# Softcap attention and MLP: q and k loaded in 128-byte runs and turned in 32x32 blocks on VectorE, scores as single float32 products, tokens in natural order

## The chip, the cores and the metric

The kernel runs on one NeuronCore of one Trainium2 chip. The metric is the time of one execution on the device, in microseconds. The kernel before has a median of 661.09 us over three runs (660.58 to 662.39).

## What is computed

Four batches of twelve heads, 448 tokens, 64 numbers per head. Attention with a soft cap on the scores, then an MLP with a squared ReLU over the 1792 tokens (768 wide, 2048 hidden). Cut to what matters:

```
scores = (1 / sqrt(64)) * q @ k.T              # q, k, v: (4, 12, 448, 64) float32
scores = cap * tanh(scores / cap)              # cap = 30
attn = exp(scores - max)                       # softmax over the keys
attn = attn / (sum(attn) + 1e-9)
x = (attn @ v), heads side by side             # (1792, 768)
h = maximum(x @ w_in, 0)                       # w_in (768, 2048), w_out (2048, 768): 8-byte floats
out = (h * h) @ w_out                          # (1792, 768) float32
```

## The kernel before, in words

Work is done by pairs of heads: 24 pairs (`NP`), six for each batch. The two heads of a pair lie in the upper and the lower 64 partitions of the array, so that one instruction of ScalarE or VectorE serves both, and a product for the one head can run on the row tiles beside that for the other.

**Loads.** `load_q`, `load_k` and `load_v` (L334 to L347) fetch one pair with four DMAs each. A head's 448 tokens are cut as 64 groups of 7 neighbours, (p t) with t = 7; group p goes to partition p, four of its seven tokens in one half of the partitions and three in the other. On the tile's side each token is a run of 64 floats, 256 bytes. This is why tokens stand in the order `ORDER` (L202), and why `put` (L752) writes each result block as two DMAs of 64 rows seven tokens apart. q is issued from SyncE (SP), k and v from GpSimd (POOL).

**Turning.** `transpose_k` and `transpose_q` (L357, L363) turn k and q with eight TensorE transposes of 128x128 into PSUM: k into a bank of `ps_t`, q into the second half of the score tile `half`. `take` (L369) then splits each into a rounded float32r part (`kqh`) and the rest (`kql`), four VectorE operations for a pair.

**Scores.** `scores(n, u)` (L378) makes scores of pair n with the keys on the partitions and the 448 queries as columns. Units u = 1, 2, 3 hold 128 keys of each head, on two row tiles of 64; unit 0 holds the last 64 keys of both heads in one product over 128 rows, where zeros that `prepare` wrote keep the heads apart. Each unit is three float32r products (hi hi, hi lo, lo hi), which add up to a float32 one. The score tiles come from `ps_s`, which has two buffers: scores(n, 0) and the transposes of q need the buffer that the tanh of scores(n, 1) reads, scores(n, 3) that of scores(n, 2).

**The rest of a pair.** `tanh` and `exp` on ScalarE (L392, L397). Then, one pair behind: `pv_half` (L404), the products with v and with ones for unit 0, four float32 products on the four 64x64 quarters of the array; `sums` (L414), the row sums; `pv` (L421), the six products with v of units 1 to 3; `evac` (L428) on ScalarE. `take_sums`, `invert`, `spread` and `normalise` bring the reciprocal of the sums back through DRAM by DMAs of SyncE and write x as a float32r part and a rest.

**The order.** Through the whole attention stage the order on each engine and queue is written out by hand in the loop at L534. For pair n TensorE does: scores 1 and 2; the transposes of pair n + 1; scores 0; from pair 9 on one part of the first MLP product (`part`, six matmuls of L309); scores 3; pv_half, sums and pv of pair n - 1. ScalarE does: tanh 1, tanh 2, exp 1, exp 2, a step of decoding, tanh 3, tanh 0, exp 3, exp 0, a step of decoding, evac. The decoding turns 8-byte weights into float32r pairs (L30), a step at a time, and fetches the weights from the SyncE queue (L272) behind the loads of q. Loads for pair n + 2 are issued in pair n, into one of two buffers (four for v).

After the 24 pairs come the rest of the first MLP product (L309, until about 443 us), whose order a planner sets, and the second (L748) by a seven-product scheme, in an order written by hand.

Of the kernel before, what the change touches and what calls it, by code (L numbers as in the profile page):

```python
# [10 lines left out]
F32 = mybir.dt.float32  # L11
F32R = mybir.dt.float32r
# [176 lines left out]
def tile_softcap_attention_mlp(ctx, tc, q, k, v, cap, w_in, w_out, out):  # L189
    nc = tc.nc  # L190
    B, H, S, D = q.shape
    NT, DM = out.shape
    DFF = w_in.shape[1]
    P = 128
    NS = S // D
    NPAIR = H // 2
    NP = B * NPAIR
    KDM = DM // P
    NF = DFF // P
    HO = DM // 2  # L200
# [6 lines left out]
    NKQ = 2  # L207
    NKV = 4
# [12 lines left out]

    hpad = rctx.enter_context(tc.tile_pool(name="hpad", bufs=1))
    hpad.tile([P, 16], F32, name="hpad")
    qp = rctx.enter_context(tc.tile_pool(name="qp", bufs=2))
    wpool = wctx.enter_context(tc.tile_pool(name="w", bufs=NEARLY, side="right"))
    scr = wctx.enter_context(tc.tile_pool(name="scr", bufs=1, side="right"))
    ps_m = rctx.enter_context(tc.tile_pool(name="ps_m", bufs=1, space=PSUM))
# [18 lines left out]

    kn = [keep.tile([P, 4, 2, D], F32, name=f"kn{i}") for i in range(NKQ)]
    qn = [keep.tile([P, 4, 2, D], F32, name=f"qn{i}") for i in range(NKQ)]  # L250
    vn = [keep.tile([P, 2, 4, D], F32, name=f"vn{i}") for i in range(NKV)]

    ones = keep.tile([P, 2, 32], F32, name="ones")
    zero = keep.tile([P, P], F32, name="zero")

    def prepare():

        for t in kn:
            nc.vector.memset(t[D:P, 3, 0], 0.0)
            nc.vector.memset(t[0:D, 3, 1], 0.0)  # L260
        for t in qn:
            nc.vector.memset(t[D:P, 3], 0.0)
        nc.vector.memset(ones[:, 0], 1.0)
        nc.vector.memset(ones[:, 1], 0.0)

# [17 lines left out]
            yield from decode_f64(nc, pool, raw, hi[:, o:o + HO], lo[:, o:o + HO], HO, bufs)  # L283

    def hold_win(f, pool, tags):
        win[f] = tuple(pool.tile([P, 4 * P + S], F32R, tag=t, name=t)[:, :DM] if tags == LATE else
                       pool.tile([P, DM], F32R, tag=t, name=t) for t in tags)
        return win[f]

    EARLY, LATE = ("whi", "wlo"), ("kqh", "kql")  # L290

    def load_wout(f, pool, scratch):
        hi = pool.tile([P, DM], F32R, tag="ohi", name="ohi")
# [30 lines left out]

    top, bottom = slice(0, D), slice(D, P)

    def load_keys(dst, src, n, queues):
        b, j = divmod(n, NPAIR)
        for i, at in enumerate((4, 3)):
            x = src[b, 2 * j + i].rearrange("(p t) d -> p t d", t=NS)  # L330
            yield queues[i].dma_start(out=dst[top, 0:at, i], in_=x[:, 0:at])  # L331
            yield queues[i].dma_start(out=dst[bottom, 0:NS - at, i], in_=x[:, at:NS])

    def load_k(n, queues=(nc.sync, nc.sync)):  # L334
        for _ in load_keys(kn[n % NKQ], k, n, queues):
            pass

    def load_q(n, upper=(nc.sync, nc.sync), lower=None):
        b, j = divmod(n, NPAIR)
        for i in range(2):  # L340
            x = q[b, 2 * j + i].rearrange("(p t) d -> p t d", t=NS)
            upper[i].dma_start(out=qn[n % NKQ][top, 0:4, i], in_=x[:, 0:4])
            (lower or upper)[i].dma_start(out=qn[n % NKQ][bottom, 0:3, i], in_=x[:, 4:7])  # L343

    def load_v(n):
        for _ in load_keys(vn[n % NKV].rearrange("p h t d -> p t h d"), v, n, (nc.gpsimd, nc.gpsimd)):
            pass  # L347
# [6 lines left out]
    kqs, tps, probs, adds, pvs, es, rds = {}, {}, {}, {}, {}, {}, {}


    def transpose_k(n):  # L357
        tps[n, 0] = ps_t.tile([P, 512], F32, tag="t", name="tp")
        kf = kn[n % NKQ].rearrange("p t h d -> p t (h d)")
        for t in range(4):  # L360
            nc.tensor.transpose(tps[n, 0][:, t * P:(t + 1) * P], kf[:, t], ident)  # L361

    def transpose_q(n, tp):  # L363
        tps[n, 1] = tp
        qf = qn[n % NKQ].rearrange("p t h d -> p t (h d)")
        for t in range(4):
            nc.tensor.transpose(tp[:, t * P:(t + 1) * P], qf[:, t], ident)  # L367

    def take(n, i, cast=nc.vector.tensor_copy):  # L369
        cols = (slice(0, 4 * P), slice(4 * P, 4 * P + S))[i]  # L370
        if i == 0:
            kqs[n] = [qp.tile([P, 4 * P + S], F32R, tag=x, name=x) for x in LATE]
        hi, lo = kqs[n]
        tp = tps.pop((n, i))[:, :cols.stop - cols.start]
        cast(out=hi[:, cols], in_=tp)
        nc.vector.tensor_sub(out=lo[:, cols], in0=tp, in1=hi[:, cols].bitcast(F32))

    def scores(n, u, sc=None):  # L378
        hi, lo = kqs[n]
        if sc is None:  # L380
            sc = ps_s.tile([P, 2, 512], F32, tag="s", name="sc")
        rows, t = ((top, bottom), u - 1) if u else ((slice(0, P),), 3)
        for s, (kx, qx) in enumerate(((hi, hi), (hi, lo), (lo, hi))):
            for h, r in enumerate(rows):
                nc.tensor.matmul(out=sc[:, h, :S], lhsT=kx[r, t * P:(t + 1) * P], rhs=qx[r, 4 * P:],  # L385
                                 start=(s == 0), stop=(s == 2))
        probs[n, u] = sc

    def tanh(n, u):
# [14 lines left out]
    def pv_half(n):  # L404
        pvs[n, 0] = ps_v.tile([P, S], F32, tag="pa", name="pa")
        pvs[n, 1] = ps_v.tile([P, S], F32, tag="pb", name="pb")
        p = probs.pop((n, 0))[:, 0]
        for h, (r, o) in enumerate(((top, bottom), (bottom, top))):
            nc.tensor.matmul(out=pvs[n, 0][r], lhsT=vn[n % NKV][r, h, 3], rhs=p[r], start=True, stop=False)  # L409
# [11 lines left out]
    def pv(n):  # L421
        for u in range(1, NU):
            p = probs.pop((n, u))
            for h, r in enumerate((top, bottom)):
                nc.tensor.matmul(out=pvs[n, 0][r], lhsT=vn[n % NKV][:, h, u - 1], rhs=p[:, h],  # L425
                                 start=False, stop=(u == NU - 1))

    def evac(n):  # L428
# [41 lines left out]
    warm = ps_t.tile([P, 512], F32, tag="t", name="warm")  # L470
    for _ in range(NWARM):
        nc.tensor.matmul(out=warm[:, :P], lhsT=zero, rhs=zero, start=True, stop=True)
    make_identity(nc, ident)
    load_k(0, (nc.sync, nc.scalar))
    load_q(0, (nc.gpsimd, nc.scalar), (nc.gpsimd, nc.sync))
    nc.gpsimd.dma_start(out=cap_sb, in_=cap.partition_broadcast(P))
    load_k(1)
    load_q(1, (nc.gpsimd, nc.gpsimd))
    prepare()
    load_v(0)  # L480
    load_v(1)
# [52 lines left out]
    for n in range(NP + 1):  # L534
        on, prep, old = n < NP, n + 1 < NP, n > 0
        more = n + 2 < NP

        if on:
            scores(n, 1)
            scores(n, 2)  # L540
            tanh(n, 1)
            tanh(n, 2)
            exp(n, 1)
            exp(n, 2)
        if more:
# [12 lines left out]
        if on:
            scores(n, 0, half)
        if prep:  # L560
            take(n + 1, 0)
            take(n + 1, 1)
        if on and parts[0][1] in decoded and n >= NPAIR * (parts[0][0] + 1) + 3:
            part()
        if n >= 2:
            invert(n - 2)

        if on:
            scores(n, 3)
            tanh(n, 3)  # L570
            tanh(n, 0)
            exp(n, 3)
            exp(n, 0)

        if old:
            pv_half(n - 1)
            sums(n - 1)
        if on:
            add_p(n)
        if old:  # L580
            take_sums(n - 1)
            pv(n - 1)
        if n >= 3:
# [128 lines left out]
    with ExitStack() as mctx:  # L712
# [189 lines left out]
```

## Time and profile before

| | us |
|---|---|
| median of three runs | 661.09 |
| the profiled execution | 661.23 |
| its span, first to last instruction | 659.5 |
| TensorE matmuls busy | 642.3 |
| VectorE busy | 477.1 |
| ScalarE busy | 355.9 |
| GpSimd busy | 113.8 |
| mean granted TensorE clock, of full | 0.993 |

An engine's busy time counts the stretches in which one of its instructions is under way. Matmuls are pipelined and their ends are modelled, so that two that follow each other overlap, and a TensorE that is shown as busy is not one that gives out results at its peak. Of the chain of work that ended last, 94% is on TensorE; 35% of the span is the first MLP product, 30% the second, 12% scores, 2% the transposes of k and 14% the products with v and the sums.

### The profile page before, as it was taken

To read this page: it belongs to the slowest core of one execution; us is meant where nothing else is said; L and a number is where in the kernel's file an instruction comes from. 1 tells how busy PE (TensorE), PEld (TensorE's weight loads), DVE (VectorE), ACT (ScalarE), POOL (GpSimd) and SP (SyncE) were. 2 spreads that over 40 slices of the span, in tenths; PEclk is the share of its full clock that TensorE was granted. 3 is DMA by queue.
4 is the path that set the end of the run, shared out by engine and by line. 5 is a ranking of instruction groups with operands and counts; after the bars stand their busy time and mean duration, and the time that the engine had idled before them with its cause. 6 is when DMAs were issued, how large, how long until landed. Compare 5 with 4: busy or idle time off the path is not lost.

```text
span 659.5 us, 10469 instructions
## 1 busy us (share of the span) xinstructions
PE 642.3 (97%) x3714; PEld 522.6 (79%) x3714; DVE 477.1 (72%) x860; ACT 355.9 (54%) x498; POOL 113.8 (17%) x201
## 2 busy tenths in 40 slices
PE   6999999999999999999999999998999999999995
PEld 5444455545554599999999999998999999999995
DVE  4678878967887456279889998913989987666651
ACT  5998988978788431355557555533444442222220
POOL 8655555534540010000000000000000000000000
PEclk9999999999999999999999999998999999999999
DMA  7346454546532251366576878729979905666611
GB/s 180 93 114 139 114 131 116 145 94 152 136 100 54 58 185 62 111 206 205 178 218 191 255 238 260 227 89 340 240 191 280 291 25 163 164 165 163 164 38 40
DMA packets 134300, 104.07 MB, mean 158 GB/s; under 512 B 40064, under 2 KB 126592, under 8 KB 134240
## 3 DMA queue, kind: packets, MB, share of 16 engines
q1 hardware_dynamic: 127376, 92.23, 49.5%
q0 software_dynamic: 6112, 10.91, 6.4%
q8 instruction: 31, 0.51, 0.3%
q10 hardware_dynamic: 752, 0.18, 0.1%
q14 instruction: 29, 0.24, 0.1%
HBM read 79.69 MB, written 23.42 MB: 156 GB/s over the span
## 4 chain that ended last, share of the span: by engine, by line
PE 94%; DMA 2%; SPq 1%; ACT 1%; DVE 1%; issue 0%; DVEq 0%
PE hps L309 35%; PE po L748 30%; PE sc L385 10%; PE pa L425 8%; PE pb L417 3%; PE pa L409 3%; PE tp L361 2%; PE sc L367 2%; DMA a<-g_dram 1%; DMA wraw<-in_moe_w_in_dram 1%; DMA qn<-in_q_dram 1%; ACT p L392 0%; SPq L318 0%; SPq L343 0%; DVE gl L738 0%
## 5 line engine op out<-in xcount | busy, mean ns | idle before, releaser
L309 PE MATMUL hps<-xs,kqh 128*128 128x448 f32 x576 | 163.5, 364 | 0.0
L748 PE MATMUL po<-th,gh 128*128 128x384 f32 x392 | 132.4, 338 | 1.6 <-ACT gh L737 1.6
L748 PE MATMUL po<-th,gl 128*128 128x384 f32 x392 | 132.6, 338 | 0.6 <-DVE gl L738 0.6
L748 PE MATMUL po<-tl,gh 128*128 128x384 f32 x392 | 132.2, 337 | 0.0
L737 ACT CAST gh<-a 128x1024 fp32r<-128x1024 f32 x49 | 51.5, 1052 | 121.3 <-PE po L748 95.7
L309 PEld LDWEIGHTS hps<-xs,kqh 128*128 128x128 f32 x576 | 108.1, 188 | 7.5
L309 PE MATMUL hps<-xs,kql 128*128 128x448 f32 x288 | 104.5, 363 | 0.0
L392 ACT ACTIVATE p<-sc,qks 128x896 f32<-128x896 f32 x96 | 82.5, 911 | 12.7 <-PE sc L385 12.6
L397 ACT ACTIVATE p<-p,cap_sb 128x896 f32<-128x896 f32 x96 | 85.7, 948 | 0.0
L738 DVE TENSOR_TENSOR gl<-a,gh 128x1024 fp32r<-128x1024 f32 x49 | 59.9, 1223 | 35.5 <-DMA a<-g_dram 22.7
L313 ACT ACTIVATE r<-hps 128x448 f32<-128x448 f32 x64 | 34.7, 542 | 76.4 <-PE hps L309 74.3
L748 PEld LDWEIGHTS po<-th,gh 128*128 128x128 f32 x392 | 74.2, 189 | 1.9 <-ACT gh L737 1.9
L748 PEld LDWEIGHTS po<-th,gl 128*128 128x128 f32 x392 | 74.0, 189 | 1.0 <-DVE gl L738 1.0
L748 PEld LDWEIGHTS po<-tl,gh 128*128 128x128 f32 x392 | 74.2, 189 | 0.0
L425 PE MATMUL pa<-p,vn 128*64 128x448 f32 x288 | 59.4, 548 | 0.0
L309 PEld LDWEIGHTS hps<-xs,kql 128*128 128x128 f32 x288 | 53.9, 187 | 5.2
L309 PE MATMUL hps<-xs,whi 128*128 128x448 f32 x192 | 54.3, 363 | 0.0
L401 DVE TENSOR_TENSOR add<-p 128x896 f32<-128x896 f32 x24 | 26.2, 1092 | 34.1 <-PE pb L417 34.1
L425 PEld LDWEIGHTS pa<-p,vn 128*64 128x64 f32 x288 | 18.5, 136 | 39.8 <-issue 39.8
L385 PE MATMUL sc<-kqh 64*128 64x448 f32 (+1 forms) x168 | 42.5, 439 | 4.6 <-ACT p L392 4.0
L385 PEld LDWEIGHTS sc<-kqh 64*128 64x128 f32 (+1 forms) x168 | 18.1, 186 | 28.7 <-ACT p L392 7.7
L331 POOL DMA_DIRECT2D vn<-in_v_dram x48 | 26.0, 541 | 82.3 <-PE pa L425 82.3
(99 smaller groups left out, 1006.4 us busy)
## 6 DMA issues: line engine op xcount, KB each, us to landing
a<-g_dram SPq DMA_DIRECT2D x56, 512.0 KB
g_dram<-r SPq DMA_DIRECT2D x64, 224.0 KB
wraw<-in_moe_w_in_dram SPq DMA_DIRECT2D x32, 384.0 KB
wraw<-in_moe_w_out_dram SPq DMA_DIRECT2D x32, 384.0 KB
rb<-rd SPq DMA_DIRECT2D x48, 112.0 KB
out_dram<-osb SPq DMA_DIRECT2D x56, 96.0 KB
vn<-in_v_dram POOLq DMA_DIRECT2D x48, 64.0 KB, 2.6
w_dram<-part SPq DMA_DIRECT2D x16, 192.0 KB
```

The source lines that it names most:

```text
L309: nc.tensor.matmul(out=ps, lhsT=w[:, c * P:(c + 1) * P], rhs=x[b, c], start=(n == 0), stop=(n == 3 * KDM - 1))
L313: nc.scalar.activation(out=r, in_=ps, func=ACTF.Relu)
L331: yield queues[i].dma_start(out=dst[top, 0:at, i], in_=x[:, 0:at])
L385: nc.tensor.matmul(out=sc[:, h, :S], lhsT=kx[r, t * P:(t + 1) * P], rhs=qx[r, 4 * P:], start=(s == 0), stop=(s == 2))
L392: nc.scalar.activation(out=p, in_=probs[n, u][:, :c, :S], func=ACTF.Tanh, scale=qks)
L397: nc.scalar.activation(out=p, in_=p, func=ACTF.Exp, scale=cap_sb)
L401: nc.vector.tensor_add(out=adds[n], in0=probs[n, 1], in1=probs[n, 2])
L409: nc.tensor.matmul(out=pvs[n, 0][r], lhsT=vn[n % NKV][r, h, 3], rhs=p[r], start=True, stop=False)
L425: nc.tensor.matmul(out=pvs[n, 0][r], lhsT=vn[n % NKV][:, h, u - 1], rhs=p[:, h], start=False, stop=(u == NU - 1))
L737: nc.scalar.copy(out=hi, in_=x)
L738: nc.vector.tensor_sub(out=lo, in0=x, in1=f32(hi))
L748: nc.tensor.matmul(out=po, lhsT=w[:, c], rhs=m[:, cols], start=(c == 0 and i == 0), stop=(c == HF - 1 and i == 2))
```

## The change

It changes how q and k are loaded, turned and multiplied, and with that the order of the tokens.

- q and k of a pair lie in one tile `kqn` of 128 partitions. `load_kq` fetches k or q with four DMAs of 32 partitions: each takes half of a head's 64 numbers (32 floats, 128 bytes), token 32 t + r to partition r. q stays on SyncE and k on GpSimd in the loop.
- `turn_kq` turns all 32x32 blocks of k and q at once, with one VectorE transpose of 128x896, into `kq`; the eight TensorE transposes and the four operations of `take` are gone.
- `scores` makes each unit as one float32 product per head. Units 1 to 3 take every third key, `kt[r, u - 1:3 * P:3]`, as the stationary operand; unit 0 is two products of 64x64, each on the rows and the columns of its own half.
- v is loaded with three DMAs: three neighbouring tokens (768 bytes) to a partition, and the last 64 tokens of each head.
- `put` writes a result block as one DMA of 128 rows.
- At the start the first loads are issued before the identity is made, and v of pair 0 comes before k and q of pair 1. The pool `qp` has four buffers of one tag where it had two of two tags.

The core of the diff:

```diff
-    def load_keys(dst, src, n, queues):
+    def load_kq(n, i, *queues):
         b, j = divmod(n, NPAIR)
-        for i, at in enumerate((4, 3)):
-            x = src[b, 2 * j + i].rearrange("(p t) d -> p t d", t=NS)
-            yield queues[i].dma_start(out=dst[top, 0:at, i], in_=x[:, 0:at])
-            yield queues[i].dma_start(out=dst[bottom, 0:NS - at, i], in_=x[:, at:NS])
+        for a in range(4):
+            h, w = divmod(a, 2)
+            x = (k, q)[i][b, 2 * j + h, :, 32 * w:32 * w + 32].rearrange("(t r) e -> r t e", r=32)
+            queues[a % len(queues)].dma_start(out=kqn[n % NKQ][32 * a:32 * a + 32, i], in_=x)
...
+        x, dst = v[b, 2 * j:2 * j + 2], vn[n % NKV]
+        nc.gpsimd.dma_start(out=dst[:, 0:6].rearrange("p (h u) d -> p h u d", h=2),
+                            in_=x[:, 0:3 * P].rearrange("h (p u) d -> p h u d", u=3))
+        for h, r in enumerate((top, bottom)):
+            nc.gpsimd.dma_start(out=dst[r, 6], in_=x[h, 3 * P:])
...
-    def scores(n, u, sc=None):
-        hi, lo = kqs[n]
-        if sc is None:
-            sc = ps_s.tile([P, 2, 512], F32, tag="s", name="sc")
-        rows, t = ((top, bottom), u - 1) if u else ((slice(0, P),), 3)
-        for s, (kx, qx) in enumerate(((hi, hi), (hi, lo), (lo, hi))):
-            for h, r in enumerate(rows):
-                nc.tensor.matmul(out=sc[:, h, :S], lhsT=kx[r, t * P:(t + 1) * P], rhs=qx[r, 4 * P:],
-                                 start=(s == 0), stop=(s == 2))
+    def turn_kq(n):
+        kqs[n] = qp.tile([P, 2 * S], F32, tag="kq", name="kq")
+        nc.vector.transpose(out=kqs[n], in_=kqn[n % NKQ].rearrange("p i t e -> p (i t e)"))
+
+    def scores(n, u):
+        sc = ps_s.tile([P, 2, 512], F32, tag="s", name="sc")
+        kt, qt = kqs[n][:, :S], kqs[n][:, S:]
+        for h, r in enumerate((top, bottom)):
+            if u:
+                w = kt[r, u - 1:3 * P:3]
+                nc.tensor.matmul(out=sc[:, h, :S], lhsT=w, rhs=qt[r], start=True, stop=True)
+            else:
+                nc.tensor.matmul(out=sc[r, 0, :S], lhsT=kt[r, 3 * P:], rhs=qt[r], start=True, stop=True)
...
-    make_identity(nc, ident)
-    load_k(0, (nc.sync, nc.scalar))
-    load_q(0, (nc.gpsimd, nc.scalar), (nc.gpsimd, nc.sync))
-    nc.gpsimd.dma_start(out=cap_sb, in_=cap.partition_broadcast(P))
-    load_k(1)
-    load_q(1, (nc.gpsimd, nc.gpsimd))
+    load_kq(0, 0, nc.sync, nc.scalar)
+    load_kq(0, 1, nc.sync, nc.scalar, nc.gpsimd, nc.gpsimd)
+    nc.gpsimd.dma_start(out=cap_sb, in_=cap.partition_broadcast(P))
+    load_v(0)
+    load_kq(1, 0, nc.gpsimd)
+    load_kq(1, 1, nc.sync)
+    load_v(1)
+    make_identity(nc, ident)
     prepare()
-    load_v(0)
-    load_v(1)
-    transpose_k(0)
-    take(0, 0, nc.scalar.copy)
-    transpose_q(0, ps_m.tile([P, 512], F32, tag="m", name="tp"))
-    take(0, 1, nc.scalar.copy)
+    turn_kq(0)
...
         if on:
-            half = ps_s.tile([P, 2, 512], F32, tag="s", name="sc")
+            scores(n, 0)
         if prep:
-            transpose_k(n + 1)
-            transpose_q(n + 1, half[:, 1])
-        if on:
-            scores(n, 0, half)
-        if prep:
-            take(n + 1, 0)
-            take(n + 1, 1)
+            turn_kq(n + 1)
...
-            for a in range(2):
-                b, blk = divmod(2 * tt + a, NS)
-                dst = out[b * S:(b + 1) * S, o * HO:(o + 1) * HO].rearrange("(p t) e -> t p e", t=NS)[ORDER[blk]]
-                nc.sync.dma_start(out=dst, in_=osb[a * D:(a + 1) * D])
+            nc.sync.dma_start(out=out[tt * P:(tt + 1) * P, o * HO:(o + 1) * HO], in_=osb)
```

## Rows read from the trace of the kernel before

**Rows 1.** Stretches; columns: length, busy by engine (instructions), clock, DMA share, GB/s.
```profile
65.89:74.07 8.18, 8.18 (x60) 3.97 (x59) 6.33 (x13) 7.62 (x10) 4.58 (x8) 1.00 0.44 116
193.87:203.25 9.38, 9.38 (x65) 5.09 (x63) 7.15 (x15) 7.72 (x10) 2.09 (x4) 1.00 0.47 118
```
**Rows 2.** Order of time, TensorE, one pair without a part: start, length, instruction.
```profile
65.89 0.47 PE L385 MATMUL sc<-kqh 64*128 64x448 f32 x2
...
67.86 0.66 PE L367 MATMUL sc<-ident,qn 128*128 128x128 f32 x4
68.27 0.45 PE L385 MATMUL sc<-kqh 128*128 128x448 f32 x1
...
69.05 0.47 PE L385 MATMUL sc<-kqh 64*128 64x448 f32 x2
...
69.86 0.59 PE L409 MATMUL pa<-p,vn 64*64 64x448 f32 x1
...
70.28 0.54 PE L409 MATMUL pa<-p,vn 64*64 64x448 f32 x1
...
70.77 0.56 PE L417 MATMUL pb<-add,ones 128*32 128x448 f32 x1
...
71.66 2.48 PE L425 MATMUL pa<-p,vn 128*64 128x448 f32 x12
74.07 0.47 PE L385 MATMUL sc<-kqh 64*128 64x448 f32 x2
```
**Rows 3.** Order of time, ScalarE, the same pair: its first two tanh.
```profile
66.80 1.91 ACT L392 ACTIVATE p<-sc,qks 128x896 f32<-128x896 f32 x2 [0.23 <-PE sc L385]
```
**Rows 4.** Order of time, TensorE, the last pair: scores(23, 0).
```profile
214.60 0.47 PE L385 MATMUL sc<-kqh 128*128 128x448 f32 x1 [0.49 <-ACT p L392]
```
**Rows 5.** Order of time, TensorE, a pair with a part: scores 0, part, scores 3.
```profile
196.25 0.45 PE L385 MATMUL sc<-kqh 128*128 128x448 f32 x1
...
196.94 0.57 PE L309 MATMUL hps<-xs,whi 128*128 128x448 f32 x2
...
198.24 0.47 PE L385 MATMUL sc<-kqh 64*128 64x448 f32 x2
```
**Rows 6.** Instructions by line and form: busy us, mean ns, idle before.
```profile
L401 DVE TENSOR_TENSOR add<-p 128x896 f32<-128x896 f32 x24 | 26.2, 1092 | 34.1 <-PE pb L417 34.1
...
L376 DVE TENSOR_TENSOR kql<-tp,kqh 128x512 fp32r<-128x512 f32 x24 | 16.6, 691 | 5.2 <-ACT kqh L375 4.4
...
L385 PEld LDWEIGHTS sc<-kqh 64*128 64x128 f32 x144 | 13.6, 185 | 27.8 <-issue 7.5 <-ACT p L392 6.9 <-ACT p L397 3.8
...
L462 DVE CAST xs<-x 128x448 fp32r<-128x448 f32 x24 | 9.5, 394 | 0.8
```
**Rows 7.** DMA issues by line: KB each, median us from issue to landing.
```profile
kn<-in_k_dram POOLq DMA_DIRECT2D x44, 64.0 KB, 3.1
```
**Rows 8.** Stretches of the start, columns as in rows 1.
```profile
4.00:6.00 2.00, 1.90 (x10) 1.40 (x9) 0.00 (x0) 0.12 (x1) 2.00 (x5) 1.00 0.79 187
...
12.00:14.00 2.00, 0.00 (x0) 0.00 (x0) 1.26 (x3) 0.73 (x3) 2.00 (x4) 1.00 1.07 353
...
16.00:18.00 2.00, 2.00 (x13) 1.33 (x10) 1.11 (x3) 2.00 (x4) 2.00 (x4) 0.50 0.78 173
```
**Rows 9.** The chain that ended last: the start, and a later pair's scores 1, 2.
```profile
2.45 3.60 DMA qn<-in_q_dram
...
6.85 0.60 SPq L342
...
9.50 4.41 DMA wraw<-in_moe_w_in_dram
...
15.43 2.50 PE sc L385 x12
...
74.14 1.41 PE sc L385 x12
```
**Rows 10.** Order of time, SyncE's queue, the last issues.
```profile
653.31 1.10 SPq L758 DMA_DIRECT2D out_dram<-osb  x2
```

More of the change, by code (lines that the diff above doesn't have):

```diff
@@ L195, in tile_softcap_attention_mlp @@
     NS = S // D
+    NT32 = S // 32
     NPAIR = H // 2
@@ L201, in tile_softcap_attention_mlp @@
     scale = 1.0 / float(D) ** 0.5
-    ORDER = (0, 4, 1, 5, 2, 6, 3)
     NEARLY = 4
@@ L223, in tile_softcap_attention_mlp @@
     hpad.tile([P, 16], F32, name="hpad")
-    qp = rctx.enter_context(tc.tile_pool(name="qp", bufs=2))
+    qp = rctx.enter_context(tc.tile_pool(name="qp", bufs=4))
     wpool = wctx.enter_context(tc.tile_pool(name="w", bufs=NEARLY, side="right"))
@@ L243, in tile_softcap_attention_mlp @@
     ps_v = actx.enter_context(tc.tile_pool(name="ps_v", bufs=1, space=PSUM))
-    kn = [keep.tile([P, 4, 2, D], F32, name=f"kn{i}") for i in range(NKQ)]
-    qn = [keep.tile([P, 4, 2, D], F32, name=f"qn{i}") for i in range(NKQ)]
-    vn = [keep.tile([P, 2, 4, D], F32, name=f"vn{i}") for i in range(NKV)]
+    kqn = [keep.tile([P, 2, NT32, 32], F32, name=f"kqn{i}") for i in range(NKQ)]
+    vn = [keep.tile([P, NS, D], F32, name=f"vn{i}") for i in range(NKV)]
     ones = keep.tile([P, 2, 32], F32, name="ones")
@@ L256, in prepare @@
     def prepare():
[L258 to L262, printed above, removed]
         nc.vector.memset(ones[:, 0], 1.0)
@@ L285, in hold_win @@
     def hold_win(f, pool, tags):
-        win[f] = tuple(pool.tile([P, 4 * P + S], F32R, tag=t, name=t)[:, :DM] if tags == LATE else
+        win[f] = tuple(pool.tile([P, 2 * S], F32R, tag=t, name="kq")[:, :DM] if tags == LATE else
                        pool.tile([P, DM], F32R, tag=t, name=t) for t in tags)
         return win[f]
-    EARLY, LATE = ("whi", "wlo"), ("kqh", "kql")
+    EARLY, LATE = ("whi", "wlo"), ("kq", "kq")
     def load_wout(f, pool, scratch):
@@ L325, in tile_softcap_attention_mlp, with load_v @@
     top, bottom = slice(0, D), slice(D, P)
-    def load_keys(dst, src, n, queues):
+    def load_kq(n, i, *queues):
         b, j = divmod(n, NPAIR)
-        for i, at in enumerate((4, 3)):
-            x = src[b, 2 * j + i].rearrange("(p t) d -> p t d", t=NS)
-            yield queues[i].dma_start(out=dst[top, 0:at, i], in_=x[:, 0:at])
-            yield queues[i].dma_start(out=dst[bottom, 0:NS - at, i], in_=x[:, at:NS])
[L334 to L338, printed above, removed]
-        b, j = divmod(n, NPAIR)
[L340 to L347, printed above, removed]
+        for a in range(4):
+            h, w = divmod(a, 2)
+            x = (k, q)[i][b, 2 * j + h, :, 32 * w:32 * w + 32].rearrange("(t r) e -> r t e", r=32)
+            queues[a % len(queues)].dma_start(out=kqn[n % NKQ][32 * a:32 * a + 32, i], in_=x)
+    def load_v(n):
+        b, j = divmod(n, NPAIR)
+        x, dst = v[b, 2 * j:2 * j + 2], vn[n % NKV]
[3 more added lines that the diff above has]
+            nc.gpsimd.dma_start(out=dst[r, 6], in_=x[h, 3 * P:])
     NU = 4
@@ L353, in tile_softcap_attention_mlp @@
     NSCR = 2
[L354 to L372, printed above, removed]
-        hi, lo = kqs[n]
-        tp = tps.pop((n, i))[:, :cols.stop - cols.start]
-        cast(out=hi[:, cols], in_=tp)
-        nc.vector.tensor_sub(out=lo[:, cols], in0=tp, in1=hi[:, cols].bitcast(F32))
-    def scores(n, u, sc=None):
-        hi, lo = kqs[n]
-        if sc is None:
-            sc = ps_s.tile([P, 2, 512], F32, tag="s", name="sc")
-        rows, t = ((top, bottom), u - 1) if u else ((slice(0, P),), 3)
-        for s, (kx, qx) in enumerate(((hi, hi), (hi, lo), (lo, hi))):
-            for h, r in enumerate(rows):
-                nc.tensor.matmul(out=sc[:, h, :S], lhsT=kx[r, t * P:(t + 1) * P], rhs=qx[r, 4 * P:],
-                                 start=(s == 0), stop=(s == 2))
+    kqs, probs, adds, pvs, es, rds = {}, {}, {}, {}, {}, {}
+    def turn_kq(n):
[10 more added lines that the diff above has]
+                nc.tensor.matmul(out=sc[r, 0, :S], lhsT=kt[r, 3 * P:], rhs=qt[r], start=True, stop=True)
         probs[n, u] = sc
@@ L408, in pv_half @@
         for h, (r, o) in enumerate(((top, bottom), (bottom, top))):
-            nc.tensor.matmul(out=pvs[n, 0][r], lhsT=vn[n % NKV][r, h, 3], rhs=p[r], start=True, stop=False)
+            nc.tensor.matmul(out=pvs[n, 0][r], lhsT=vn[n % NKV][r, 6], rhs=p[r], start=True, stop=False)
             nc.tensor.matmul(out=pvs[n, 1][o], lhsT=ones[r].rearrange("p a c -> p (a c)"), rhs=p[r],
@@ L424, in pv @@
             for h, r in enumerate((top, bottom)):
-                nc.tensor.matmul(out=pvs[n, 0][r], lhsT=vn[n % NKV][:, h, u - 1], rhs=p[:, h],
+                nc.tensor.matmul(out=pvs[n, 0][r], lhsT=vn[n % NKV][:, 3 * h + u - 1], rhs=p[:, h],
                                  start=False, stop=(u == NU - 1))
@@ L545, in tile_softcap_attention_mlp @@
         if more:
-            load_q(n + 2)
-            load_k(n + 2, (nc.gpsimd, nc.gpsimd))
+            load_kq(n + 2, 0, nc.gpsimd)
+            load_kq(n + 2, 1, nc.sync)
             load_v(n + 2)
```

## The prediction

> **What bounds the kernel now.** I read the table of stretches first, to see which engine has no time left in the attention stage, then the order of time on TensorE and on ScalarE inside one head pair, then the chain of waits at the start, and the end. In a pair of attention the table shows TensorE busy for 8.18 of 8.18 us, ScalarE for 7.62, VectorE for 6.33, GpSimd for 4.58 and the DMA engines at 0.44; in a pair that also carries a part of the MLP TensorE is busy for all of 9.38 us [rows 1]. A full TensorE would mean that every matmul taken out is time won. The order of time says otherwise, and the reader should follow it step by step [rows 2, 3]: scores(n, 1) starts at 65.89; its tanh (I call it T1) starts at 66.80, 0.91 later; the transposes of q start at 67.86, 1.06 after T1 started; scores(n, 0) at 68.27, scores(n, 3) at 69.05, pv_half at 69.86, the sums at 70.77, pv at 71.66, and the next scores(n, 1) at 74.07. The 1.06 is a wait: the q transposes and scores(n, 0) write the PSUM buffer that T1 reads. In the last pair, which has no transposes to fill it, it stands open: 0.49 us of idle before scores(n, 0), put down to the tanh [rows 4]. So the period is a loop through ScalarE: 0.91 + 1.06 + 0.41 + 0.78 + 0.81 + 0.91 + 0.89 + 2.41 = 8.18. The k transposes and scores(n, 2) lie beside the wait, and cost nothing.
>
> From about 226 us on TensorE is full of MLP products that the change does not touch. I expect nothing there, except that the orders the planner finds and the handover at about 445 us may shift by a microsecond or two either way.
>
> **The score products.** Before, a unit (one call of scores) is three float32r products, two row tiles side by side: 0.81 us for scores(n, 3) with its change of tiling. After, a unit is one float32 product on two row tiles. The nearest row is pv_half, float32 on 64-row tiles: its second pass starts 0.42 after the first (70.28 after 69.86), lasts 0.54, and the next unit starts 0.91 after it [rows 2]. So I take 0.91 for a unit alone, and for scores(n, 1) 0.42 + 0.54 + 0.05 = 1.01 until T1 can start (0.05 as now). The bounds: 0.80 if the change of tiling cost nothing (pv's twelve passes, two at a time, take 2.41: 0.40 a step, two steps a unit); 1.71 if the two row tiles ran one after the other (a rival below). T1 itself does not change. The q transposes leave the loop (-0.41), the k transposes leave a place beside it. scores(n, 2) follows scores(n, 1) in one tiling and is done after some 1.7 us, inside the 1.01 + 1.06 that scores(n, 0) must wait for. scores(n, 3) needs the second tanh, which ends 0.9 after the first, just when scores(n, 0) is over.
>
> Without a part the loop becomes 1.01 + 1.06 + 0.91 + 0.91 + 0.91 + 0.89 + 2.41 = 8.10, by 0.08 less; eight pairs (1 to 8), -0.6 us. With a part the old step from scores(n, 0) to the part is 0.69 and from the part to scores(n, 3) 1.30 [rows 5]. After: +0.10 (T1 later) - 0.41 (q transposes) + 0.22 (0.91 for 0.69) + 0.11 (0.91 for 0.80, scores(n, 3)) = +0.02; fourteen pairs, +0.3. The last pair had no transposes to lose: +0.4. All pairs together: +0.1. TensorE does much less after the change, but what it saves turns into a wait for T1. ScalarE, with 7.62 of 8.1 us, has room, so no new bound comes from there.
>
> **Weights.** scores(n, 1) to (n, 3) now read the stationary operand in steps of three floats. A load of 128 contiguous columns takes 185 ns [rows 6], under the 0.40 us of a float32 step, so it is hidden but for the first of a unit. No row shows a load with a step. Below, a step costs nothing; above, I let it double the load, as a rival. I take nothing.
>
> **VectorE.** Four operations per pair, of at most 691 ns, go; one transpose of 128x896 comes. The nearest rows are a copy of 448 columns at 394 ns (0.8 us for 896) and an addition of 896 columns at 1092 [rows 6]. I take 1.0; four times that, 4 us, would still fit, since VectorE has 6.33 of 8.18 filled, of which 2.6 go. It is hidden in every pair but the first. The new instruction waits for eight loads, and behind it on VectorE stand the inversion, the sum of probabilities and the copy of the sums, for which pv_half of the next pair waits. The loads can be issued once the transpose two pairs earlier has read the buffer, well over 8 us ahead; a k load lands 3.1 us after its issue [rows 7]. GpSimd issues seven DMAs for eight at 4.58 / 8 = 0.57 us each, so 4.0; SyncE four as now.
>
> **The loads.** Per pair, k and q are 3584 pieces of 128 bytes where there were 1792 of 256; v falls from 896 pieces of 256 to 256 of 768 and 128 of 256. From 4 to 6 us, with such loads alone, the engines moved 187 GB/s at a share of 0.79 [rows 8]: 237 GB/s when full, 17 ns per piece of 256 bytes on each of 16 engines. A piece of 128 costs between 8.6 (by bytes) and 17 ns (by pieces); I take 11. For k and q that makes 1.9 to 3.8 us of all engines per pair for 1.9 now; with 0.44 x 8.18 = 3.6 us in use, at most 5.5 of 8.1: not a bound between pairs.
>
> **The start.** The chain is [rows 9]: the loads of q land at 6.05; SyncE's four loads for pair 2 are issued from 6.85, the first weights at 9.50, landing 4.41 us later; the decode on ScalarE waits for them with the tanh behind it, so pair 1 starts at 15.43, at half clock (12 score products in 2.50 us, where 1.41 is what they have at full clock; granted clock 0.50 from 16 to 18 us [rows 8], the 1.2 GHz level, after a stretch from 12 to 14 us without a matmul). After: k and q of pair 0 land 0 to 1.9 us later than 6.05; the transpose takes 1.0 where the step over TensorE, 6.05 to 6.85, took 0.80; only then is the buffer free for pair 2, 2.65 us of issues follow, then the weights. That is +0.2 to +2.1, and these transfers run while the engines are full (share 1.07 from 12 to 14 us [rows 8]), which adds 0 to 2. At 11 ns a piece the two are +0.8 and +0.5; TensorE's longer units at half clock add 0.2. I take +1.5, between -1 (v in larger pieces empties the queue sooner) and +4.
>
> The Trainium skill, "DMA: Bandwidth & Descriptors", Specifications, asks for 512 bytes or more per transfer for full rate; by rows 8 the 256-byte pieces indeed stay at 237 GB/s, against 353 from 12 to 14 us, when the weights' pieces of 1024 bytes ran too. Its rule has no figure for 128 bytes; halving once more would be the upper end above.
>
> **The end.** The last result goes out as two DMAs, 1.10 us of issue for both [rows 10]; one is left: -0.55.
>
> **Sum**, against the profiled execution's 661.23 us (its span is 659.5, and 1.7 lie outside): +1.5 (start) + 0.1 (pairs) - 0.55 (end) = +1.05. The median shown is 661.09, 0.14 below it: 662.1.
>
> **Rivals.**
> 1. The start comes out ahead. For it: a matmul, a copy and a subtraction between the landing of q and the first score become one operation, and v's larger pieces leave the queues sooner. The start is then -1, and if the change of tiling costs 0.05 us less in each of scores(n, 0) and scores(n, 3), half of what lies between 0.80 and 0.91, the 24 pairs give another 2.4: -1 - 0.55 + 0.1 - 2.4, so 657.3. Against it: the weights still wait behind the transpose.
> 2. Slower: weights with a step. If a load takes 0.37 instead of 0.185, the first load of scores(n, 1) and of scores(n, 3), which nothing covers after a change of tiling, adds 0.19 each to the loop: 0.38 x 24 = 9, so 671. It decides once the exposed load exceeds 0.185 by more than some 0.03 (24 x 2 x 0.03 = 1.5 us). For it: these are the only loads with such a step; against it: no row has one. The Trainium skill, "SBUF — State Buffer", Door 1: The DMA port swizzle, speaks of 16-byte lines that want at least two accesses each for full rate; a step of 12 bytes gives 1.33. It agrees in sign with this rival, and no run here shows its size.
> 3. Slower: small pieces cost 17 ns or more. The start is then +4, and a pair whose loads land late stalls VectorE now and then: 664.5 to 667.
> 4. The row tiles of a float32 product run one after the other. Three units of the loop become 0.80 longer: 2.4 x 24 = 58, so 720. Against it: pv_half runs four float32 tiles side by side [rows 2].
>
> **Chances.** Forecast 0.42, its own range 660 to 663.5; rival 1 0.22; rival 2 0.16; rival 3 0.17; rival 4 0.03. About 0.3% (2 us) is what a measurement here can tell from none: faster than 659.1 is most of rival 1, 0.21; within is most of the forecast and a little of rivals 1 and 3, 0.43; slower is rivals 2 to 4 and the forecast's upper end, 0.36. The range, 656.5 to 671, leaves out rival 4 and the ends of 1 and 2.
>
> **What would show it.** In the changed kernel's order of time a pair without a part should have scores(n, 1) to T1 at 1.0, T1 to scores(n, 0) at 1.06 with some 0.4 us of idle before it put down to the tanh, and a period near 8.1; 9.4 with a part. Pair 1 should start near 17 us. A load of score weights near 185 ns puts rival 2 out; the spacing of two units of scores shows rival 4. If the period is under 7.9, T1 is not in the loop as I say, and the forecast is wrong on the fast side.

## The result, and the profile after

The changed kernel takes 668.22 us (median of 4 runs, 667.1 to 668.94), beside 661.66 for the kernel before on the same chip (4 runs, 660.58 to 662.39): 1.010 times the time, 95% interval 1.0082 to 1.0117. It is slower, by 6.6 us, inside the range and on the slow side of the forecast of 662.1. The profiled execution says the same: its span is 666.1 us, 6.6 more than before.

Stretches of the changed kernel: a pair without a part, a pair with one, and three of the start (columns as in [rows 1]).

```profile
66.03:74.35 8.32, 7.96 (x46) 2.70 (x44) 4.78 (x10) 7.61 (x10) 4.32 (x7) 1.00 0.64 114
168.65:178.37 9.72, 9.36 (x52) 3.74 (x51) 6.00 (x12) 7.75 (x10) 4.33 (x7) 1.00 0.68 139
...
8.00:10.00 2.00, 2.00 (x6) 0.83 (x6) 0.27 (x2) 1.67 (x2) 1.93 (x5) 0.50 0.86 151
...
12.00:14.00 2.00, 1.16 (x6) 0.43 (x4) 0.00 (x0) 2.00 (x5) 2.00 (x4) 1.00 1.10 364
...
16.00:18.00 2.00, 1.53 (x8) 0.68 (x6) 1.97 (x4) 2.00 (x3) 2.00 (x4) 1.00 0.70 132
```

A pair takes 8.32 us where it took 8.18, and TensorE is no longer full in it: 7.96 of 8.32. TensorE has less to do and the pair is longer, so the time is in a wait. VectorE fell from 6.33 to 4.78.

Order of time on TensorE in the changed kernel: the pair without a part, then the pair with one (start, length, instruction, in brackets the idle time before it and what ended it).

```profile
66.03 1.84 PE L353 MATMUL sc<-kq 64*128 64x448 f32 x8
68.23 0.97 PE L355 MATMUL sc<-kq 64*64 64x448 f32 x4 [0.35 <-ACT p L361]
69.13 1.09 PE L353 MATMUL sc<-kq 64*128 64x448 f32 x4
70.15 0.59 PE L378 MATMUL pa<-p,vn 64*64 64x448 f32 x1
...
71.06 0.56 PE L386 MATMUL pb<-add,ones 128*32 128x448 f32 x1
...
71.95 2.48 PE L394 MATMUL pa<-p,vn 128*64 128x448 f32 x12
74.35 1.84 PE L353 MATMUL sc<-kq 64*128 64x448 f32 x8
...
168.65 1.84 PE L353 MATMUL sc<-kq 64*128 64x448 f32 x8
170.84 0.97 PE L355 MATMUL sc<-kq 64*64 64x448 f32 x4 [0.36 <-ACT p L361]
171.74 0.68 PE L303 MATMUL hps<-xs,whi 128*128 128x448 f32 x2
...
173.15 1.09 PE L353 MATMUL sc<-kq 64*128 64x448 f32 x4
```

The same pair on ScalarE: its first two tanh.

```profile
67.17 1.91 ACT L361 ACTIVATE p<-sc,qks 128x896 f32<-128x896 f32 x2 [0.49 <-PE sc L353]
```

Read beside [rows 2, 3], the loop is now: scores(n, 1) to T1 1.14 (it was 0.91), T1 to scores(n, 0) 1.06 (the same, the last 0.35 of it now open idle put down to the tanh), scores(n, 0) 0.90 (the q transposes with it were 0.41 + 0.78), scores(n, 3) 1.02 (0.81), pv_half 0.91, sums 0.89, pv 2.40 as before. Sum 8.32. In the pair with a part, the part takes 1.41, from 171.74 to 173.15, where it took 1.30 [rows 5].

Instructions by line and form, beside [rows 6] (busy us, mean ns, idle before):

```profile
L353 PEld LDWEIGHTS sc<-kq 64*128 64x128 f32 x288 | 33.1, 253 | 39.7 <-ACT p L361 11.0 <-issue 7.5 <-ACT p L366 4.2
...
L345 DVE STREAM_TRANSPOSE kq<-kqn 128x896 f32<-128x896 f32 x24 | 26.6, 1106 | 5.7 <-DMA kqn<-in_q_dram 5.4 <-DMA wraw<-in_moe_w_in_dram 0.2
```

A load of 128 score weights takes 253 ns; it took 185.

The chain of waits at the start, beside [rows 9]:

```profile
2.11 4.33 DMA kqn<-in_q_dram
...
6.52 1.11 DVE kq L345
...
7.69 3.35 PE sc L353 x8
...
11.97 1.96 ACT p L366 x2
...
14.02 0.43 ACT mag L44
14.46 1.41 ACT p L361 x2
```

SyncE's queue, beside [rows 9, 10]: the first weights, and the last issue.

```profile
9.59 1.01 SPq L266 DMA_DIRECT2D wraw<-in_moe_w_in_dram  x2
...
659.65 0.33 SPq L715 DMA_DIRECT2D out_dram<-osb  x1
```

Where the 6.6 us are, place by place. The sums of pair 0 start at 21.14 (21.74 before): -0.6. From there to the sums of pair 23 (228.63, and 223.23 before) it is 207.49 us for 201.49: +6.0. That is nine intervals without a part at 8.32 for 8.17 (+0.15 each), eleven with one at 9.73 for 9.38 (+0.34), the one with the scores of the last pair (9.73 for 8.98), a single longer one that both kernels have (10.98 for 10.85), and the last, 4.91 in both. From there to the last issue of the output 431.0 for 430.1: +0.9, of which about 0.4 lie ahead of the second MLP product and 0.5 at the handover, where TensorE waits 2.19 us for a cast on ScalarE (1.61 before). From that issue to the end 6.45 for 6.19: +0.3.

So nearly all of it is in the pairs, which were to give +0.1.

### The profile page after: what moved, and what is told of

The parts are those of the page before. It is cut to its first block, busy times and chain, and to the rows that moved or that the text cites. A ratio compares the mean times of both kernels' runs of the same rounds, so it can differ in the third digit from the quotient of the medians.

```text
span 666.1 us, 9652 instructions
## 1 busy us (share of the span) xinstructions
PE 639.3 (96%) x3402; PEld 490.1 (74%) x3402; DVE 443.0 (67%) x784; ACT 354.3 (53%) x496; POOL 108.2 (16%) x177
## 4 chain that ended last, share of the span: by engine, by line
PE 89%; ACT 5%; DMA 3%; DVE 1%; issue 1%; SPq 0%; POOL 0%; DVEq 0%; POOLq 0%
PE hps L303 34%; PE po L708 30%; PE pa L394 8%; PE sc L353 7%; ACT p L361 4%; PE sc L355 3%; PE pb L386 3%; PE pa L378 3%; DMA a<-g_dram 1%; DMA wraw<-in_moe_w_in_dram 1%; DMA kqn<-in_q_dram 1%; ACT p L366 1%; SPq L312 0%; DVE gl L698 0%; DVE x L428 0%
## 5 line engine op out<-in xcount | busy, mean ns | idle before, releaser
L303 PE MATMUL hps<-xs,kq 128*128 128x448 f32 x864 | 174.9, 364 | 0.0
L303 PEld LDWEIGHTS hps<-xs,kq 128*128 128x128 f32 x864 | 162.1, 188 | 12.6
L353 PE MATMUL sc<-kq 64*128 64x448 f32 x288 | 71.7, 604 | 5.3 <-DVE qks L452 2.7
L326 POOL DMA_DIRECT2D kqn<-in_k_dram x92 | 58.5, 643 | 28.7 <-DVE cmp L411 24.9
L353 PEld LDWEIGHTS sc<-kq 64*128 64x128 f32 x288 | 33.1, 253 | 39.7 <-ACT p L361 11.0
L303 PE MATMUL hps<-xs,whi 128*128 128x448 f32 x192 | 55.7, 371 | 0.1
L303 PEld LDWEIGHTS hps<-xs,whi 128*128 128x128 f32 x192 | 34.9, 188 | 12.5 <-issue 7.8
L714 DVE TENSOR_TENSOR osb<-s,po 128x384 f32<-128x384 f32 x28 | 15.5, 553 | 33.8 <-PE po L708 33.6
```

Source lines behind the costliest of these rows:

```text
L303: nc.tensor.matmul(out=ps, lhsT=w[:, c * P:(c + 1) * P], rhs=x[b, c], start=(n == 0), stop=(n == 3 * KDM - 1))
L326: queues[a % len(queues)].dma_start(out=kqn[n % NKQ][32 * a:32 * a + 32, i], in_=x)
L353: nc.tensor.matmul(out=sc[:, h, :S], lhsT=w, rhs=qt[r], start=True, stop=True)
```

## The experiments

The theory after the result (A in the expectations): the load of weights in steps of three floats is longer, nothing covers the first load of scores(n, 1) and of scores(n, 3), and so each excess stands twice in the loop. Its rival B: a float32 unit on 64x128 tiles costs the excess by itself, whatever the step.

**Contiguous weights in the changed kernel.** Tokens on partitions in the order of the first kernel, so that the score weights are contiguous; the first 384 tokens of v then take two DMAs of 256-byte pieces per pair of heads where one with 768-byte pieces stood, so it is not the step alone that changes.

```diff
-                w = kt[r, u - 1:3 * P:3]
+                w = kt[r, (u - 1) * P:u * P]
 ... (in load_v, for each head h, in place of the DMA with 768-byte runs)
+            nc.gpsimd.dma_start(out=dst[:, 3 * h:3 * h + 3], in_=x[h, 0:3 * P].rearrange("(u p) d -> p u d", p=P))
```

> The changed kernel, but scores(n, 1) to (n, 3) read 128 contiguous columns of k as stationary operand instead of every third; v is loaded to match, in pieces of 256 bytes with four DMAs, so the result is the same. Theory A (the step of three floats makes a load of weights longer, 248 ns for 185, and the first load of scores(n, 1) and of scores(n, 3) has no cover): loads at 185 ns, scores(n, 1) to its tanh 1.02 us instead of 1.14, scores(n, 3) 0.91 instead of 1.02, periods 8.10 and 9.50 for 8.32 and 9.73, about 5.3 us less than the changed kernel: 663. Rival B (the float32 unit on two row tiles of 64x128 costs that by itself, with its four loads of 128 columns): periods stay at 8.32 and 9.73, 668.

665.86 us beside 660.87: ratio 1.0086 (1.0059 to 1.0113). The loads of units 1 to 3 and of unit 0, by line and form:

```profile
L352 PEld LDWEIGHTS sc<-kq 64*128 64x128 f32 x288 | 24.3, 189 | 43.1 <-issue 15.9 <-ACT p L360 11.3 <-ACT p L365 4.2
...
L354 PEld LDWEIGHTS sc<-kq 64*64 64x64 f32 x96 | 4.7, 131 | 27.8 <-ACT p L360 27.8
```

Its order of time, TensorE, a pair without a part:

```profile
65.39 1.77 PE L352 MATMUL sc<-kq 64*128 64x448 f32 x8
67.52 0.97 PE L354 MATMUL sc<-kq 64*64 64x448 f32 x4 [0.36 <-ACT p L360]
68.42 1.02 PE L352 MATMUL sc<-kq 64*128 64x448 f32 x4
69.38 0.59 PE L377 MATMUL pa<-p,vn 64*64 64x448 f32 x1
...
73.58 1.77 PE L352 MATMUL sc<-kq 64*128 64x448 f32 x8
```

And ScalarE's first tanh of that pair:

```profile
66.46 1.91 ACT L360 ACTIVATE p<-sc,qks 128x896 f32<-128x896 f32 x2 [0.39 <-PE sc L352]
```

The load is back at 189 ns, 0.064 us less; scores(n, 1) to T1 is 1.07 for 1.14, scores(n, 3) 0.96 for 1.02, the pair 8.19 for 8.32, the pair with a part 9.60 for 9.73. The step costs 0.13 us in every pair, two loads' excess, as theory A has it. But 8.19 is not the 8.10 that I had without a step: 0.06 in scores(n, 1) and 0.05 in scores(n, 3) remain. That is left to theory B; the part on the prediction comes back to it. The total gained 2.4 us on the changed kernel; the two intervals overlap, so by the totals alone this gain would not be certain.

**Steps of two and of four floats in the changed kernel.**

```diff
-                w = kt[r, u - 1:3 * P:3]
+                w = kt[r, u - 1:u - 1 + 2 * P:2]      (and in the second: kqs[n][r, u - 1:u - 1 + 4 * P:4])
```

> The changed kernel, with a step of two floats in place of three in the stationary operand of scores(n, 1) to (n, 3). The units then hold other keys than they should; everything else is computed as before. Theory A with lines of 16 bytes that want two accesses: two per line, loads at 185 ns, periods 8.10 and 9.50, 663. Theory A with a price on any step: about 215 ns, period 8.2, 665.5. Rival B: 8.32 and 668.

> The changed kernel, with a step of four floats in place of three in the stationary operand of scores(n, 1) to (n, 3) (the columns run on into those of q, so the scores are of other vectors than they should be). Theory A with lines of 16 bytes: one access per line, 128 lines for 96; if the price grows with the lines beyond 64, loads at about 315 ns, 0.11 us more in each of two units, period 8.55 and 9.95, 673.5. Theory A with one flat price for a step that leaves the line: 248 ns, 8.32, 668. Rival B: 8.32 and 668.

The units of both read other keys than they should, and do the same work. 665.1 and 671.39 us, one run each, beside the same 660.87. The loads, step of two first:

```profile
L353 PEld LDWEIGHTS sc<-kq 64*128 64x128 f32 x288 | 25.3, 196 | 42.8 <-issue 15.3 <-ACT p L361 11.3 <-ACT p L366 4.2
```

```profile
L353 PEld LDWEIGHTS sc<-kq 64*128 64x128 f32 x288 | 41.2, 313 | 37.2 <-ACT p L361 11.2 <-issue 7.5 <-ACT p L366 4.2
```

The pairs take 8.21 and 8.44 us (9.62 and 9.84 with a part). With the contiguous run and the changed kernel that makes four points: a load of 189, 196, 253, 313 ns gives 8.19, 8.21, 8.32, 8.44. From 189 to 313 the load grows by 0.124 and the pair by 0.25: two loads per pair, within 0.01. That is what theory A says, and it has no other free number.

How the load grows with the step: from one float to two it costs 7 ns, from two to three 57, from three to four 60. The Trainium skill, "SBUF — State Buffer", Door 1: The DMA port swizzle, says that a line of 16 bytes wants two accesses or more for full rate. By that rule steps of one and two are free and steps of three (1.33 accesses a line) and four (one) are not; these four loads agree but for the 7 ns. The same passage gives four float32 as the distance that is still free, and there the 313 ns disagree: the measurement decides.

**A step of three in the kernel before.** The float32r products of scores 1 to 3 read their weights with the step; the keys of the three units are then mixed, the work is the same.

```diff
-                nc.tensor.matmul(out=sc[:, h, :S], lhsT=kx[r, t * P:(t + 1) * P], rhs=qx[r, 4 * P:],
+                w = kx[r, t:3 * P:3] if u else kx[r, t * P:(t + 1) * P]
+                nc.tensor.matmul(out=sc[:, h, :S], lhsT=w, rhs=qx[r, 4 * P:],
```

> The kernel before, with every third column of k as stationary operand of scores(n, 1) to (n, 3) (the keys of the three units are then mixed among each other; all the work is there). The disputed cost by itself, on float32r products. Theory A: loads at 248 ns for 185; scores(n, 1) to its tanh 1.0 for 0.91, scores(n, 3) 0.9 for 0.81, period 8.4 for 8.18 and 9.6 for 9.39, 5 us more than the kernel before; 3 us more still if the loads cannot follow each other every 0.2 us. Rival B: loads or periods as in the kernel before, 661.

664.6 us, ratio 1.0052 (1.0035 to 1.0069); pairs 8.32 and 9.54 us for 8.17 and 9.38. The load, by line and form:

```profile
L386 PEld LDWEIGHTS sc<-kqh 64*128 64x128 f32 x144 | 18.1, 248 | 27.7 <-issue 7.2 <-ACT p L393 7.0 <-ACT p L398 4.1
```

Its scores(n, 3), in order of time:

```profile
70.96 0.54 PE L386 MATMUL sc<-kqh 64*128 64x448 f32 x2
...
71.83 0.59 PE L410 MATMUL pa<-p,vn 64*64 64x448 f32 x1
```

0.87 from scores(n, 3) to pv_half where [rows 2] have 0.81. The step alone, put into a kernel with nothing else of the change, makes it slower by 0.15 us a pair, where twice the longer load (248 ns for 185) makes 0.13. So the price is not one of float32 products alone.

**Filling the wait.** If the pair is a loop through the tanh with 0.35 us of idle in it, work moved into the idle time is free. pv_half of the pair before, 0.91 us, depends on nothing in this pair. In the changed kernel it goes ahead of scores(n, 0):

```diff
+        if old:
+            pv_half(n - 1)
         if on:
             scores(n, 0)
 ...
         if old:
-            pv_half(n - 1)
             sums(n - 1)
```

> The changed kernel, with pv_half of pair n - 1 moved on TensorE from behind scores(n, 3) to before scores(n, 0). Theory A (TensorE waits for the tanh of scores(n, 1), some 0.36 us of idle in each pair, and pays a change of tiling before and after each float32 unit): pv_half fills the wait and shares the 64x64 tiling with scores(n, 0), so the period falls from 8.32 to 1.77 + 1.68 + 1.02 + 0.89 + 2.41 = 7.77 and from 9.73 to 9.2, and the time by about 12 us to 656. Rival C (ScalarE, with 7.6 us of work in a pair, is the bound once TensorE is relieved): no lower than about 8.0 and 9.3, 660 to 662. Rival D (the wait shown is no part of the loop): 8.32, 668.

654.98 us beside 661.43, ratio 0.9886 (0.9859 to 0.9912). Order of time, TensorE:

```profile
70.20 1.84 PE L353 MATMUL sc<-kq 64*128 64x448 f32 x8
...
71.97 0.59 PE L378 MATMUL pa<-p,vn 64*64 64x448 f32 x1
...
72.77 0.93 PE L355 MATMUL sc<-kq 64*64 64x448 f32 x4
73.62 1.09 PE L353 MATMUL sc<-kq 64*128 64x448 f32 x4
...
77.94 1.84 PE L353 MATMUL sc<-kq 64*128 64x448 f32 x8
```

The pair takes 7.74 us, 0.58 less, and one with a part 9.15, again 0.58 less; the idle time before scores(n, 0) is gone. One move of a unit gives more than the whole change cost (0.15 and 0.34 a pair), and puts out the rivals that the wait was not part of the loop (D in the expectations) and that ScalarE holds a pair at 8.0 (C). Not all of the 0.58 is the wait. From scores(n, 1) to the next unit it is 1.77 us (70.20 to 71.97) where it was 2.20 (66.03 to 68.23): 0.43. The rest comes from the order: pv_half and scores(n, 0), both on 64x64 tiles and now neighbours, take 0.80 and 0.85 for 0.91 and 0.90.

**Contiguous weights and pv_half in the wait together.** The two edits above.

> The changed kernel with both edits: contiguous stationary operands (as e1_contiguous) and pv_half before scores(n, 0) (as e5_pvhalf_first). Theory A: 1.70 + 1.68 + 0.96 + 0.89 + 2.41 = 7.64 without a part and 9.05 with one, some 12 us less than e1_contiguous: 653 to 654, faster than the kernel before by 1%. Rival C: 7.9 and 9.2, 657. Rival D: as e1_contiguous, 665.9.

651.17 us beside 661.43, ratio 0.983 (0.9805 to 0.9854): faster than both kernels, and apart from the run before, so the step is seen in the total too. Order of time, TensorE:

```profile
69.75 1.77 PE L352 MATMUL sc<-kq 64*128 64x448 f32 x8
71.45 0.59 PE L377 MATMUL pa<-p,vn 64*64 64x448 f32 x1
...
72.25 0.93 PE L354 MATMUL sc<-kq 64*64 64x448 f32 x4
```

The stretch of that pair:

```profile
69.75:77.36 7.61, 7.61 (x47) 2.43 (x46) 5.45 (x11) 7.50 (x10) 5.13 (x8) 1.00 0.79 125
```

7.61 us, TensorE without a gap and ScalarE at 7.50. Here both are nearly full; to shorten a pair without a part by more than 0.1 us, work has to go from both. Pairs with a part take 9.02.

**The part in the wait**, with contiguous weights: part() goes ahead of scores(n, 0), pv_half stays where it was.

```diff
+        if on and parts[0][1] in decoded and n >= NPAIR * (parts[0][0] + 1) + 3:
+            part()
         if on:
             scores(n, 0)
 ... (and not behind it)
```

> e1_contiguous with the part of the MLP product moved from behind scores(n, 0) to before it, into the wait for the tanh. Theory A: pairs without a part stay at 8.19, pairs with one fall from 9.60 to 1.70 + 1.41 + 0.90 + 0.96 + 0.91 + 0.89 + 2.41 = 9.18, 14 pairs, 6 us: 660, about as fast as the kernel before. Rival D: 9.60 and 666.

658.6 us beside 661.43, ratio 0.9944 (0.9921 to 0.9968). Order of time, TensorE, a pair with a part:

```profile
171.99 1.77 PE L352 MATMUL sc<-kq 64*128 64x448 f32 x8
173.69 0.67 PE L303 MATMUL hps<-xs,whi 128*128 128x448 f32 x2
...
175.10 0.97 PE L354 MATMUL sc<-kq 64*64 64x448 f32 x4
...
181.16 1.77 PE L352 MATMUL sc<-kq 64*128 64x448 f32 x8
```

Pairs with a part 9.17 us for 9.60, those without as in the contiguous run, 8.19. Only the pairs with something in the wait gain, and they gain 0.43: what the wait gave to pv_half, with nothing from the order.

**pv_half in the wait, in the kernel before**: between its transposes of k and of q.

> The kernel before with pv_half of pair n - 1 moved between the transposes of k and those of q: the control for e5_pvhalf_first. Theory A: in the kernel before the transposes fill the wait for the tanh, so there is nothing to fill: 8.18 and 9.39 as before (only the 0.14 us between the end of the k transposes and the tanh could go), 659 to 661. If an earlier pv_half helped for any other reason, the period would fall here as well, by 0.4 to 0.5 us, to 650.

660.03 us beside 661.43, ratio 0.9969 (0.9948 to 0.9989). Order of time, TensorE:

```profile
66.48 0.47 PE L385 MATMUL sc<-kqh 64*128 64x448 f32 x2
...
67.90 0.66 PE L361 MATMUL tp<-ident,kn 128*128 128x128 f32 x4
68.49 0.59 PE L409 MATMUL pa<-p,vn 64*64 64x448 f32 x1
...
74.69 0.47 PE L385 MATMUL sc<-kqh 64*128 64x448 f32 x2
...
215.22 0.47 PE L385 MATMUL sc<-kqh 128*128 128x448 f32 x1
```

The pair stays at 8.21 us (8.17 before): there the k transposes already fill the wait. In the last pair, which has no transposes and where [rows 4] show 0.49 us of idle before scores(23, 0), the same move does gain: no idle is left there (215.22), and from sums to sums it is 8.45 us for 8.98. So the move helps where the wait is open and not elsewhere, and the 1.7% of the best version is not the move alone; the change made the room that the move fills. Its profiled execution (span 660.6) is not shorter than that of before (659.5) either, so I build nothing on the 0.3% of the total.

**Two output DMAs of 64 rows in the changed kernel**, as the kernel before has them.

```diff
-            nc.sync.dma_start(out=out[tt * P:(tt + 1) * P, o * HO:(o + 1) * HO], in_=osb)
+            for a in range(2):
+                nc.sync.dma_start(out=out[tt * P + a * D:tt * P + (a + 1) * D, o * HO:(o + 1) * HO], in_=osb[a * D:(a + 1) * D])
```

> The changed kernel with each result block written as two DMAs of 64 rows again (rows in natural order). From the end of the last addition to the end of the span it is 6.48 us in the changed kernel and 6.21 in the kernel before. If one DMA of 128 rows takes that much longer to finish than two of 64, the end goes back to 6.2 us; if it is the place of the rows in memory, it stays at 6.5. The pairs do not change: 8.32 and 9.73.

667.03 us, one run. SyncE's last issues:

```profile
659.03 1.11 SPq L716 DMA_DIRECT2D out_dram<-osb  x2
```

From 659.03 to its span's end at 665.2 it is 6.2 us, as in the kernel before (653.31 to 659.5: 6.19), and 6.45 with one DMA. The other traces bear it out: the four that end with two DMAs take 6.15 to 6.19 from there, the seven that end with one 6.37 to 6.84. One DMA is issued sooner and ends later.

## Why the prediction came out as it did

The sum was +1.05 (start +1.5, pairs +0.1, end -0.55); the spans differ by +6.6 (start -0.6, pairs +6.0, middle and handover +0.9, end +0.3). The time lies in the range because the range took in rival 2. That it came this far up is partly luck: rival 2 alone, at the size that it had, would have given about 665, and two further terms in the pairs that the prediction did not have, with the middle and the end, make up the rest, less a start that came out ahead. What the forecast had wrong is what the first load of a unit costs.

**The loop was right.** T1 to scores(n, 0) stayed at 1.06 with 0.35 us of idle put down to the tanh; the k transposes cost nothing before and won nothing when they went; the q transposes gave their 0.41; scores(n, 0) takes 0.90 where 0.91 was forecast; what TensorE saves became a wait. The moves of pv_half and of the part, which fill this wait and gain 0.43 by it, are the test of it.

**The step that failed: "No row shows a load with a step. ... I take nothing."** Rival 2 is what happened, at a third of its size: the load is 253 ns, not 370, and its excess of 0.064 stands twice in the loop: 0.13 x 22 intervals = 2.9 us. The prediction's own point of decision, an excess of 0.03, was passed twice over; the chance of 0.16 was too low for a case that had no row against it.

**A second term of the same kind: the first load without a step.** I took a unit's 0.91 from pv_half, whose loads are of 64 columns (pv's, also 64 columns, take 136 ns); the score loads are of 128, 189 ns. The difference, 0.053, is close to the 0.06 and 0.05 that scores(n, 1) and scores(n, 3) have above the forecast with contiguous weights. scores(n, 0) bears it out: it is a float32 unit behind a change of tiling too, its loads have 64 columns and take 131 ns in the contiguous run, and it takes 0.90 there where scores(n, 3) takes 0.96. Its tiles are 64x64, though, not 64x128, so the columns are not all that differs, and no run changes them alone. Twice 0.055 x 22 is 2.4 us, nearly as much as the step. Both durations lay in the trace of before: a unit's first load was named as exposed, and its length was then not put in.

**A part behind a unit of small tiles.** From scores(n, 0) to the part 0.90 came as forecast; that the part itself would take 1.41 for 1.30 did not. Before, it followed products on whole 128x128 tiles; after, products on 64x64 tiles, and in the run with the part first 64x128 tiles, again 1.41. 0.11 in each of eleven pairs and in the last, 1.3 us. That the tiling ahead of it is the cause is argued from these three places; no run changes it alone. (The prediction counted eight pairs without a part and fourteen with one; the trace has two more of the first kind, in the middle, which changes its sum by about 0.2 us.)

Pair by pair these terms close the sum. Without a part: forecast -0.08, and 0.13 + 0.11 makes +0.16; it measured +0.15. With a part: forecast +0.02, and 0.13 + 0.11 + 0.11 makes +0.37; it measured +0.34. The interval of the last pair: forecast +0.4, with 0.35 it is +0.75, as measured. The single longer interval, +0.13, got less, because in it T1 does not wait for scores(n, 1): ScalarE stands before a cast of the decoding, idle for 2.61 us in both kernels, and what follows T1 starts 3.44 us after scores(n, 1) in both (the q transposes before, scores(n, 0) after). The terms behind T1 alone give +0.15.

**The start was wrong in its sum and, at its end, in its chain** (+1.5, came -0.6). The loads landed at 6.44, 0.4 later than q before; the transpose took 1.11; the buffer was free at 7.66 for 6.85. But from there to the weights it is 1.93 us for 2.65, so they were issued at 9.59 for 9.50. And this chain does not wait for them: the decode finds them there at 13.92, when ScalarE comes to it, and the chain runs from the slow score products of pair 0 (3.35 us) through tanh and exp to the tanh at 14.46, for 14.48 before. In other runs of this start, that with two output DMAs among them, the wait for the weights is still in the chain, so the two are nearly equal.

What the half clock costs moved: before, TensorE had no matmul from 12 to 14 us and the granted clock was 0.50 from 16 to 18 [rows 8]; after, it has 1.16 us of work from 12 to 14, the clock is 0.50 from 8 to 10 and 1.00 from 16 to 18. The change alone does not settle that. Of the eight traces with the new start five have a clock of 0.50 from 8 to 10 us, one (two output DMAs) from 18 to 20, and two (the changed kernel with pv_half in the wait, the run with the part in the wait) show 1.00 from 8 to 20. The first sums of these traces and of the three with the old start lie between 20.5 and 22.8 us, so the half microsecond itself is not to be read closely.

**The end**: the issue is indeed 0.33 for 1.10, and nothing came of it: from the issue to the end of the span it is longer by 0.3.

**Pieces.** The DMA share of 0.64 x 8.32 = 5.3 us per pair is near the upper end (5.5): by this estimate, which takes the rest of a pair's transfers as before, a piece of 128 bytes costs nearly as much engine time as one of 256. That is the price of rival 3, but not its effect: k lands 3.5 us after its issue for 3.1 [rows 7], no matmul of the pairs waits for it, and the start did not lose 4 us. Of rival 1 the start came ahead, and its gain in the pairs did not. Rival 4 did not come: a unit takes 0.90.

## What to carry to other kernels

Where a loop waits for another engine, work taken out ahead of the wait only widens it; look for a unit with no tie to the loop and put it into the wait, and with that and contiguous weights the same change turned from 1.0% slower to 1.7% faster. Ask of every first weight load behind a change of tiling how many columns it has and with what step they lie, since nothing covers it. Where no row prices an operation that the loop holds twice per turn, a sum that takes it at nothing is the weakest term, and its rival deserves the larger chance.

## What the runs showed of the hardware

- A load of 128 float32 weight columns on 64 rows takes 189, 196, 253, 313 ns at steps of 1, 2, 3, 4 floats; the same step of three costs float32r weights 248.
- A part of the same products takes 1.41 us behind products on 64x64 or 64x128 tiles and 1.30 behind those on 128x128. A float32 unit on 64x64 tiles takes 0.80 to 0.86 next to another such unit and 0.90 to 0.91 otherwise.
- A transpose of 128x896 float32 in 32x32 blocks takes VectorE 1106 ns, as an addition of that size does (1092 [rows 6]).
- One output DMA of 128 rows is issued in 0.33 us, two of 64 rows in 1.10; from that issue to the end it is 6.37 to 6.84 us with the one (seven traces) and 6.15 to 6.19 with the two (four).
